# Linear attention into a routed expert layer on one core: TensorE's attention stages issued in pairs of steps, and the 1e-6 of the denominators added by ScalarE

## The chip, the core and the metric

The kernel runs on one core of a Trainium2 chip. The metric is device time in microseconds (us) of one execution; the time before the change is 609.04 us, the median of three runs (607.51 to 610.86). Five engines matter: TensorE (PE in the profile, its weight loads PEld), VectorE (DVE), ScalarE (ACT), GpSimd (POOL), and SyncE (SP), which here only issues DMAs. Each engine runs its own instructions strictly in the order in which they stand in the program; engines wait for one another through semaphores.

## The reference, cut to what matters

Inputs q, k and v are (8, 8, 576, 64): 8 batches, 8 heads, 576 rows, 64 columns. In short:

```python
def phi(x):
    proj = x @ w_phi                                  # 64 -> 128 features
    proj = proj - max(abs(proj), axis=-1)
    return concat([exp(proj), exp(-proj)])            # 256 features
q_p, k_p = phi(q), phi(k)
kv = k_p.T @ v                                        # per batch and head
z  = sum(k_p over rows)
attn = (q_p @ kv) / (q_p @ z + 1e-06)
x = attn with the heads side by side                  # (4608, 512)
do_compute = x @ w_skip > 0
expert = argmax(x @ w_gate)                           # 8 experts
out = x, and for rows with do_compute:
      x + gate * (relu(x @ w1[expert]) @ w2[expert])
```

The change lies in the attention. The expert layer follows it and is not edited.

## The kernel before, in words

**Units and items.** The work of the attention is cut into 32 units: for each of the 8 batches, two groups of four heads for k and two for q. A unit is cut into five items, numbered 0 to 4: item 0 is the last 64 rows of each head (the tail), items 1 to 4 are quarters of the other 512 rows. Two streams of 80 items, one of k and one of q, run through the same pipeline; the q stream runs 6 steps behind the k stream.

**Steps.** A loop counts steps t. In each step every stage handles the item that its lag gives. The stages are called in the order of the string `EPAZUT`, after which come the loads of v:

- T (lag 0): VectorE transposes raw rows into xT (lines 322 and 324).
- P (lag 1): TensorE multiplies xT with w_phi into ps_P (line 347). VectorE then takes the largest absolute value (354) and subtracts it (357), which gives u. ps_P has two buffers. With two full items the product is 1024 columns wide, with a tail 768.
- E (lag 3): for k, ScalarE takes the two exponentials of u (372, 373), which gives ek, and GpSimd adds parts of ek into z (380 to 386). For q, TensorE first transposes u into ps_U (393; a single buffer), and ScalarE takes the exponentials from there (399, 400).
- U (lag 4): for k, TensorE adds ek against v into ps_K (415, 422); after item 4 ScalarE copies the sum out as kvs (426). For q, TensorE multiplies the exponentials with kva into ps_O (513; the tail of odd batches at 492), and then `norm` divides: VectorE adds 1e-6 to the four denominators of a row (den, 464), takes the reciprocal (468) and multiplies twice (475, 476, tiles xm and lgm).
- Z (lag 5, item 4 of k only): TensorE sums z over the rows (433), ScalarE copies it out as zs (436).
- A (lag 6, item 4 of k only): TensorE multiplies kvs with a constant matrix that also holds the gate weights (446) and appends zs (450), in two halves; ScalarE copies each half out as kva (451, 454).

ps_O has two buffers, and the results of U, Z, the two halves of A and some small products of the router all take turns in them.

**A batch takes ten steps.** Z falls on steps that end in 4 or 9, A on those that end in 0 or 5. At a step that ends in 9 a batch of q is complete, and the router's small VectorE operations (lines 568 to 642) are queued for the steps after it.

**Who sets the order.** From step 8 to step 78 TensorE's instructions stand as the loop emits them (a manual schedule for that engine alone). The order of the other engines is set by a scheduler that plays the program through ahead of time, and the buffers of a pool are handed out by the same scheduler.

Of the kernel before, what the change touches and what calls it, by code (L numbers as in the profile page):

```python
# [12 lines left out]
AF = mybir.ActivationFunctionType  # L13
ALU = mybir.AluOpType
# [4 lines left out]
P = 128  # L19
SLOT = 256  # L20
CFG = {'late': 1, 'gp': (0, 1, 2, 4, 6, 8, 9, 11, 12, 14, 17, 19, 21), 'rows': 9.0, 'tab': (2, 4, 5, 6, 6, 7, 8, 9, 10, 11, 12, 13, 16, 20, 32), 'ql': -2, 'q1': 0, 'vtl': 3, 'at': 6, 'cp': 0, 'seq': ('E', 'E', 'E', 'C', 'C', 'SC', 'C', 'DS', 'C', 'D'), 'lag': (1, 3, 4, 5, 6), 'post': (4, 7, 7), 'man': (8, 79), 'dnow': 0, 'off': 6, 'order': 'EPAZUT', 'direct': (), 'nb': {'K': 1, 'P': 3, 'U': 2, 'O': 2}, 'na': {'K': 1, 'P': 2, 'U': 1, 'O': 2}, 'apools': (('ld', 2), ('hl', 5), ('up', 3), ('zp', 2), ('ep', 7), ('kvp', 6), ('ac', 1), ('xp', 2)), 'mpools': (('rawp', 1), ('mx', 2), ('wseta', 1), ('mo', 2), ('wsetb', 1), ('rawq', 1))}
# [3 lines left out]
def kernel(  # L25
# [12 lines left out]
    nc = tc.nc  # L38
    B, H, S, D = q.shape
    NF = w_phi.shape[1]  # L40
    E = w_gate.shape[1]
# [10 lines left out]
    NAUG = D + E + 2  # L52
    NA1 = NAUG - 1
# [80 lines left out]
    def setup_aug():  # L134
        nc.gpsimd.memset(aug, 0.0)
        for hd in range(2):
            r = slice(hd * D, (hd + 1) * D)
            c = hd * NA1
            for g in range(NP2):
                nc.gpsimd.tensor_copy(out=aug[r, g, c:c + D], in_=ident[r, hd * D:(hd + 1) * D])  # L140
            nc.gpsimd.tensor_copy(out=aug[r, :, c + D:c + NA1], in_=wgs[r])
# [114 lines left out]
    with actx:  # L256
# [17 lines left out]
        for b in range(B):  # L274
            for kind in ("k", "q"):
                for hq in range(NQ):
                    u = Unit()
# [9 lines left out]
        def st_load(u):  # L287
            src = kv_in[u.kind]
            u.raw = ld.tile([P, 2, 18, 32], F32, tag="raw", name="raw", bufs=6)
            for hd in range(2):  # L290
                for dh in range(2):
                    r = hd * 64 + dh * 32
                    nc.sync.dma_start(
                        out=u.raw[r:r + 32].rearrange("p r t c -> p (r t) c"),
                        in_=src[u.g, hd][:, :, dh * 32:dh * 32 + 32])

        def st_loadv(u):
            u.v = ld.tile([P, 4, 4 * D], F32, tag="v", name="v", bufs=3)
            u.vt = vts[u.g % 3]
            for h in range(4):  # L300
                nc.sync.dma_start(
                    out=u.v[:, h, :].rearrange("p (g c) -> p g c", c=D),
                    in_=vu[u.g, 0:4 * P, h, :].rearrange("(g p) c -> p g c", p=P))

        def st_loadvt(u):
            for pr in range(2):
                r = slice(pr * 64, pr * 64 + 64)
                nc.sync.dma_start(
                    out=u.vt[r, pr], in_=vu[u.g, 4 * P:S].rearrange("p (n r) c -> p r n c", r=2)[:, pr])
# [17 lines left out]
        def st_proj():  # L327
            todo = []
            for items, us, off in streams:
                s = now[0] - off - LP  # L330
                if 0 <= s < n:
                    todo.append(items[s])
            if not todo:
                return
            todo.sort(key=lambda x: x[1] == 0)
            p = psa.tile([P, 2, 512], F32, tag="P", name="ps_P", bufs=CFG["na"]["P"])
            nj = 0
            spans = []
            for u, i in todo:
                xT = u.hlp[0 if i == 0 else (i + 1) // 2]  # L340
                m = 1 if i == 0 else 2
                for j in range(m):
                    g = 0 if i == 0 else 2 * ((i - 1) % 2) + j
                    for hd in range(2):
                        r = slice(hd * 64, hd * 64 + 64)
                        for s in range(2):
                            nc.tensor.matmul(  # L347
                                p[s * 64:s * 64 + 64, hd, (nj + j) * NF:(nj + j + 1) * NF],
                                xT[r, g * P + s * 64:g * P + s * 64 + 64], wsrc[r], start=True, stop=True)
                spans.append((u, i, 2 * nj, 2 * (nj + m)))  # L350
                nj += m
            pv = p.rearrange("p h (j f) -> p j h f", f=NF)[:, 0:nj]
            m = small.tile([P, 8], F32, tag="m", name="m")[:, 0:2 * nj]
            nc.vector.tensor_reduce(  # L354
                out=m.rearrange("p (j h) -> p j h", h=2), in_=pv, axis=AX.X, op=ALU.max, apply_absolute_value=True)
            uu = up.tile([P, 8, NF], F32, tag="u", name="u")
            nc.vector.tensor_tensor(  # L357
                out=uu[:, 0:2 * nj, :].rearrange("p (j h) f -> p j h f", h=2), in0=pv,
                in1=m.rearrange("p (j h o) -> p j h o", h=2, o=1).broadcast_to([P, nj, 2, NF]), op=ALU.subtract)
            for u, i, a, b in spans:  # L360
                u.u[i] = uu[:, a:b, :]
# [98 lines left out]
        def norm(o, xdst, ldst, shape):  # L460

            den = small.tile([P, 4], F32, tag="den", name="den")
            rec = small.tile([P, 4], F32, tag="rec", name="rec")
            nc.vector.tensor_scalar(
                out=den.rearrange("p (t o) -> p t o", o=1), in0=o[:, :, NA1:NAUG],
                scalar1=1e-6, scalar2=None, op0=ALU.add,
            )
            nc.vector.reciprocal(out=rec, in_=den)
            rv = rec.rearrange("p (t o) -> p t o", o=1)
            a, c = shape  # L470

            def sh(x):
                return x.rearrange("p (a c) d -> p a c d", a=a)

            nc.vector.tensor_tensor(out=xdst, in0=sh(o[:, :, 0:D]), in1=sh(rv.broadcast_to([P, 4, D])), op=ALU.mult)
            nc.vector.tensor_tensor(  # L476
                out=ldst, in0=sh(o[:, :, D:NA1]), in1=sh(rv.broadcast_to([P, 4, NA1 - D])), op=ALU.mult)
# [241 lines left out]
        later = []  # L719
        now = [0]  # L720
# [5 lines left out]
        LP, LE, LU, LZ, LA = CFG["lag"]  # L726
        OFF = CFG["off"]
        streams = [(x[0], x[1], 0 if j == 0 else OFF) for j, x in enumerate(streams)]
        for dh in range(2):
            nc.scalar.dma_start(  # L730
                out=wsrc[dh * 64:dh * 64 + 64],
                in_=w_phi)
# [3 lines left out]
        def run_stage(lag, f):  # L736
            for items, us, off in streams:
                s = now[0] - off - lag
                if 0 <= s < n:
                    f(*items[s])  # L740
# [7 lines left out]
        def f_t():  # L748
            for items, us, off in streams:
                s = now[0] - off  # L750
                if s == CFG["ql"]:
                    st_load(us[0])
                if 0 <= s < n:
                    u, i = items[s]
                    st_t(u, i)
                    if i == 0 and s // 5 + 1 < len(us):
                        st_load(us[s // 5 + 1])

        man = None
        for t in range(n + OFF + LA):  # L760
            if CFG["man"] and t == CFG["man"][0]:
                man = ExitStack()
                man.enter_context(tc.manual_schedule(engines={mybir.EngineType.PE}))
            if CFG["man"] and t == CFG["man"][1]:
                man.close()
            now[0] = t
            for w, f in [x for x in later if x[0] <= t]:
                later.remove((w, f))
                f()
            for c in CFG["order"]:  # L770
                if c == "Z":
                    run_stage(LZ, st_z)
                elif c == "A":
                    run_stage(LA, st_aug)
                elif c == "U":
                    run_stage(LU, f_use)
                elif c == "E":
                    run_stage(LE, f_exp)
                elif c == "P":
                    st_proj()  # L780
                else:
                    f_t()
            run_stage(LU - 3, lambda u, i: st_loadv(u) if (i == 0 and u.kind == "k") else None)
            run_stage(CFG["vtl"], lambda u, i: st_loadvt(u) if (i == 0 and u.kind == "k") else None)
            if t == CFG["at"]:
                setup_aug()
            if t == 1:
                setup()
# [310 lines left out]
    for grp in CFG["seq"]:  # L1099
# [7 lines left out]
        for which, w, n in how:  # L1107
            for _ in range(n):
                x = slots[which]
                c = done.get((x, w), 0)  # L1110
# [6 lines left out]
    order = sorted(begin, key=begin.get)  # L1117
# [27 lines left out]
    T, ready, parted = [], [], []  # L1145
# [46 lines left out]
    with tc.manual_schedule():  # L1192
# [4 lines left out]
        for k, (w, x, c) in enumerate(steps):  # L1197
            kind, i = x
# [95 lines left out]
```

## Time and profile before

One execution was profiled. Its own time was 607.91 us, 1.1 us under the median of 609.04; its span, from the first to the last instruction, is 605.7 us, and 2.2 us lie around it.

| | |
|---|---|
| time, median of 3 runs | 609.04 us |
| time of the profiled execution | 607.91 us |
| its span | 605.7 us |
| VectorE busy | 502.6 us (83%) |
| ScalarE busy | 330.7 us (55%) |
| GpSimd busy | 375.9 us (62%) |
| attention, about | 0 to 341 us |
| steps 8 to 77, about | 25 to 301 us |

In the profile, a row of the timeline gives the start in us from the beginning of the span, the duration, the engine, the line of the kernel, the operation, the tile written and the tiles read, shapes, and how many instructions are merged in the row. A note in square brackets is idle time of that engine just before the row, and what ended it; "issue" stands for time in which the engine waited for nothing that the profile shows. For TensorE, `64*64`, `128*64`, `128*128` and `128*32` name the part of the array that a matmul uses. Matmuls overlap, so the distance between the starts of two rows says more than a duration.

### The profile page before, as it was taken

To read this page: it belongs to the slowest core of one execution; us is meant where nothing else is said; L and a number is where in the kernel's file an instruction comes from. 1 tells how busy PE (TensorE), PEld (TensorE's weight loads), DVE (VectorE), ACT (ScalarE), POOL (GpSimd) and SP (SyncE) were. 2 spreads that over 40 slices of the span, in tenths; PEclk is the share of its full clock that TensorE was granted. 3 is DMA by queue.
4 is the path that set the end of the run, shared out by engine and by line. 5 is a ranking of instruction groups with operands and counts; after the bars stand their busy time and mean duration, and the time that the engine had idled before them with its cause. 6 is when DMAs were issued, how large, how long until landed. Compare 5 with 4: busy or idle time off the path is not lost. (4 is left out here: it accounts for less than half of the span.)

```text
span 605.7 us, 18767 instructions
## 1 busy us (share of the span) xinstructions
PE 567.1 (94%) x7486; PEld 466.3 (77%) x7486; DVE 502.6 (83%) x1085; ACT 330.7 (55%) x649; POOL 375.9 (62%) x399
## 2 busy tenths in 40 slices
PE   4799999999999899998989799899999998999993
PEld 2477777777777677776766699798998987988892
DVE  5799998999999989999998749956788887867841
ACT  3366565555555565564643645344557765656720
POOL 5665585495666775847865644995576674738021
PEclk9999999999999999999999999899999999999997
DMA  9998898896677567621235297489677788868500
GB/s 159 156 164 149 182 194 179 163 211 121 149 160 155 138 135 170 158 74 46 73 120 185 69 302 277 167 278 321 201 260 240 242 288 297 269 198 261 194 19 30
DMA packets 250233, 108.33 MB, mean 179 GB/s; under 512 B 192417, under 2 KB 235553, under 8 KB 250144
## 3 DMA queue, kind: packets, MB, share of 16 engines
q1 hardware_dynamic: 245632, 97.58, 62.1%
q0 software_dynamic: 3200, 9.45, 4.3%
q8 instruction: 60, 0.98, 0.7%
q10 hardware_dynamic: 1312, 0.08, 0.1%
q14 instruction: 29, 0.24, 0.1%
HBM read 83.86 MB, written 24.02 MB: 178 GB/s over the span
## 5 line engine op out<-in xcount | busy, mean ns | idle before, releaser
L380 POOL TENSOR_TENSOR z<-ek 128x512 f32<-128x512 f32 x64 | 81.2, 1272 | 77.0 <-ACT ek L373 54.3
L200 POOL TENSOR_TENSOR w<-wraw_c,w 128x256 fp32r<-128x256 f32 x108 | 97.5, 935 | 47.5 <-ACT w L195 43.9
L195 ACT ACTIVATE w<-wraw_c 128x1024 fp32r<-128x1024 f32 x96 | 97.9, 1051 | 6.9 <-DMA wraw_c<-in_moe_w_dram 6.5
L200 DVE TENSOR_TENSOR w<-wraw_c,w 128x1024 fp32r<-128x1024 f32 x69 | 90.2, 1321 | 9.5 <-ACT w L195 7.6
L354 DVE TENSOR_REDUCE m<-ps_P 128x8 f32<-128x1024 f32 (+2 forms) x86 | 88.5, 1030 | 7.1 <-PE ps_P L347 7.1
L357 DVE TENSOR_TENSOR u<-ps_P,m 128x1024 f32<-128x1024 f32 (+2 forms) x86 | 88.8, 1032 | 2.9
L347 PE MATMUL ps_P<-wsrc,xT 64*64 64x128 f32 x2048 | 79.4, 282 | 11.4 <-DMA raw<-in_k_dram 7.2
L513 PEld LDWEIGHTS ps_O<-kva,eq 128*64 128x64 f32 x2048 | 74.0, 136 | 16.4 <-issue 5.8
L513 PE MATMUL ps_O<-kva,eq 128*64 128x74 f32 x2048 | 77.4, 228 | 3.9 <-DVE lgm L476 3.8
L347 PEld LDWEIGHTS ps_P<-wsrc,xT 64*64 64x64 f32 x2048 | 57.4, 135 | 28.1 <-issue 19.2
L399 ACT ACTIVATE eq<-ps_U 128x512 f32<-128x512 f32 x64 | 37.9, 592 | 64.8 <-PE ps_U L393 64.3
L415 PE MATMUL ps_K<-ek,v 128*64 128x256 f32 x512 | 71.2, 396 | 0.0
L879 POOL DMA_INDIRECT out_dram<-o,si x22 | 34.3, 1558 | 56.6 <-DVE si L878 50.1
L946 PE MATMUL ps_O<-w,hh 128*128 128x512 f32 x160 | 64.0, 400 | 0.0
L633 POOL TENSOR_SCALAR OP<-iota_p,rkp,wcol 128x128 bf16<-128x128 f32 x62 | 48.4, 790 | 24.0 <-DVE RKH L636 17.9
L372 ACT ACTIVATE ek<-u 128x512 f32<-128x512 f32 x64 | 40.4, 631 | 39.0 <-DVE u L357 23.0
L393 PE MATMUL ps_U<-ident,u 128*128 128x128 f32 x288 | 48.9, 287 | 2.7 <-DVE u L357 2.4
L324 DVE STREAM_TRANSPOSE xT<-raw 128x512 f32<-128x512 f32 x64 | 44.7, 702 | 6.1 <-DMA raw<-in_k_dram 3.3
L415 PEld LDWEIGHTS ps_K<-ek,v 128*64 128x64 f32 x512 | 32.0, 137 | 21.1 <-issue 10.8
L950 PE MATMUL ps_O<-w,hh 128*128 128x512 f32 x120 | 47.2, 394 | 0.1
L951 PE MATMUL ps_O<-w,hlo 128*128 128x512 f32 x120 | 47.0, 392 | 0.0
L384 POOL TENSOR_TENSOR z<-z 128x512 f32<-128x512 f32 x32 | 40.7, 1273 | 2.5
(254 smaller groups left out, 1202.0 us busy)
## 6 DMA issues: line engine op xcount, KB each, us to landing
wraw_c<-in_moe_w_dram SPq DMA_DIRECT2D x96, 512.0 KB, 5.4
raw<-in_k_dram SPq DMA_DIRECT2D x64, 144.0 KB, 3.1
raw<-in_q_dram SPq DMA_DIRECT2D x64, 144.0 KB, 4.5
v<-in_v_dram SPq DMA_DIRECT2D x64, 128.0 KB, 2.8
out_dram<-xm SPq DMA_DIRECT2D x16, 512.0 KB, 6.2
xrows<-xm SPq DMA_DIRECT2D x8, 516.0 KB, 3.8
xrows<-xm SPq DMA_DIRECT2D x8, 512.0 KB, 4.2
vt<-in_v_dram SPq DMA_DIRECT2D x32, 32.0 KB, 2.5
```

The source lines that it names most:

```text
L195: nc.scalar.activation(out=hi, in_=raw, func=AF.Copy)
L200: eng.tensor_tensor(out=lo[:, r], in0=raw[:, r], in1=hi[:, r].bitcast(F32), op=ALU.subtract)
L347: nc.tensor.matmul(p[s * 64:s * 64 + 64, hd, (nj + j) * NF:(nj + j + 1) * NF], xT[r, g * P + s * 64:g * P + s * 64 + 64], wsrc[r], start=T ...
L354: nc.vector.tensor_reduce(out=m.rearrange("p (j h) -> p j h", h=2), in_=pv, axis=AX.X, op=ALU.max, apply_absolute_value=True)
L357: nc.vector.tensor_tensor(out=uu[:, 0:2 * nj, :].rearrange("p (j h) f -> p j h f", h=2), in0=pv, in1=m.rearrange("p (j h o) -> p j h o", h ...
L380: zeng.tensor_tensor(out=z, in0=e[:, 0:2, :], in1=e[:, 2:4, :], op=ALU.add)
L393: nc.tensor.transpose(t[:, tt * P:(tt + 1) * P], uu[:, tt, :], ident)
L415: nc.tensor.matmul(o[hd * 64:hd * 64 + 64, :], u.v[:, 2 * hd + pr, g * D:(g + 1) * D], u.e[i][:, 2 * j + hd, :], start=(g == 0), stop=False,)
L513: nc.tensor.matmul(ov[s * 64:s * 64 + 64, 2 * j + hd, :], e[:, half, j, hd, s * 64:s * 64 + 64], kva[:, half, 2 * pr + hd, :], start=(half ...
L633: (nc.vector if last else nc.gpsimd).tensor_scalar(out=OP[:, t0 + t, c, :], in0=iota_p, scalar1=rkp[:, t:t + 1], scalar2=wcol[:, NT:NT + 1 ...
L946: nc.tensor.matmul(y[sub], hh[:, t], wh[:, fi, :], start=first, stop=False)
L950: nc.tensor.matmul(y[sub], hh[:, t], wl[:, fi, :], start=False, stop=False)
```

## The change

The loop still counts steps. From step 8 to step 77 it now takes two steps at once and calls their stages in the order of a list, where the number is 0 for the first step of the pair and 1 for the second (L is what a step does first, the postponed stores and router products; D the loads of v). Steps 8 and 9 are the first pair; the pairs of a batch of ten steps are called 8-9, 0-1, 2-3, 4-5 and 6-7 here, after the last digit of their steps. In `norm`, the addition of 1e-6 moves from VectorE to ScalarE.

```diff
@@ norm
-            nc.vector.tensor_scalar(
-                out=den.rearrange("p (t o) -> p t o", o=1), in0=o[:, :, NA1:NAUG],
-                scalar1=1e-6, scalar2=None, op0=ALU.add,
-            )
+            nc.scalar.activation(
+                out=den.rearrange("p (t o) -> p t o", o=1), in_=o[:, :, NA1:NAUG], func=AF.Copy, bias=1e-6)
             nc.vector.reciprocal(out=rec, in_=den)
@@ the loop over steps
+        PAIR = [('L', 0), ('T', 0), ('T', 1), ('E', 0), ('P', 0), ('P', 1), ('L', 1), ('E', 1), ('A', 0), ('Z', 0), ('Z', 1), ('U', 0), ('A', 1), ('U', 1), ('D', 0), ('D', 1)]
...
-            now[0] = t
-            for w, f in [x for x in later if x[0] <= t]:
-                later.remove((w, f))
-                f()
-            for c in CFG["order"]:
-                if c == "Z":
+            first = 8 <= t < 78 and (t - 8) % 2 == 0
+            if 8 <= t < 78 and not first:
+                continue
+            for c, dt in PAIR if first else [(c, 0) for c in "L" + CFG["order"] + "D"]:
+                now[0] = t + dt
+                if c == "L":
+                    for w, f in [x for x in later if x[0] <= now[0]]:
+                        later.remove((w, f))
+                        f()
+                elif c == "Z":
                     run_stage(LZ, st_z)
```

Below is what this makes of the order on the engines, at the places of which the prediction speaks. After the change the lines that follow `norm` have numbers lower by two (511 for 513, 490 for 492).

TensorE, steps 24 and 25 (pair 4-5), before: transposes of E (L393), products of P (L347), Z (L433), q's product of U (L513), then step 25 with E, P, the two halves of A (L446, L450) and k's product of U (L415).

```order
L393 MATMUL ps_U<-ident,u 128x128 x2
L347 MATMUL ps_P<-wsrc,xT 64x128 x16
L433 MATMUL ps_O<-z,ones_f 32x256 x4
L513 MATMUL ps_O<-kva,eq 64x74 x16
L393 MATMUL ps_U<-ident,u 128x128 x4
L347 MATMUL ps_P<-wsrc,xT 64x128 x16
L446 MATMUL ps_O<-aug,kvs 128x146 x2
L450 MATMUL ps_O<-ident,zs 128x128
L446 MATMUL ps_O<-aug,kvs 128x146 x2
L450 MATMUL ps_O<-ident,zs 128x128
L415 MATMUL ps_K<-ek,v 64x256 x4
```

The same two steps on TensorE after:

```order
L393 MATMUL ps_U<-ident,u 128x128 x2
L347 MATMUL ps_P<-wsrc,xT 64x128 x32
L393 MATMUL ps_U<-ident,u 128x128 x4
L433 MATMUL ps_O<-z,ones_f 32x256 x4
L511 MATMUL ps_O<-kva,eq 64x74 x16
L446 MATMUL ps_O<-aug,kvs 128x146 x2
L450 MATMUL ps_O<-ident,zs 128x128
L446 MATMUL ps_O<-aug,kvs 128x146 x2
L450 MATMUL ps_O<-ident,zs 128x128
L415 MATMUL ps_K<-ek,v 64x256 x4
```

The products of both steps stand side by side, and nothing but q's product of U is left between Z and A; before, E and P of the next step stood there.

VectorE, steps 24 and 25, before (the numbers tell buffers apart; ps_P_2188 is the product of step 24, ps_P_2256 that of step 25):

```order
L354 TENSOR_REDUCE m_2205<-ps_P_2188 128x8
L324 STREAM_TRANSPOSE xT_2518<-raw_1935 128x512
L357 TENSOR_TENSOR u_2207<-ps_P_2188,m_2205 128x1024
L464 TENSOR_SCALAR den_2233<-ps_O_2216 128x4
L468 RECIPROCAL rec_2234<-den_2233 128x4
L475 TENSOR_TENSOR xm_1995<-ps_O_2216,rec_2234 128x4x64
L476 TENSOR_TENSOR lgm_1997<-ps_O_2216,rec_2234 128x2x18
L324 STREAM_TRANSPOSE xT_2606<-raw_2008 128x512
L354 TENSOR_REDUCE m_2273<-ps_P_2256 128x8
L357 TENSOR_TENSOR u_2275<-ps_P_2256,m_2273 128x1024
```

VectorE, the same steps after (ps_P_2197 is the product of step 24, ps_P_2218 that of step 25):

```order
L354 TENSOR_REDUCE m_2214<-ps_P_2197 128x8
L324 STREAM_TRANSPOSE xT_2455<-raw_1881 128x512
L324 STREAM_TRANSPOSE xT_2457<-raw_1890 128x512
L357 TENSOR_TENSOR u_2216<-ps_P_2197,m_2214 128x1024
L354 TENSOR_REDUCE m_2235<-ps_P_2218 128x8
L357 TENSOR_TENSOR u_2237<-ps_P_2218,m_2235 128x1024
L466 RECIPROCAL rec_2279<-den_2278 128x4
L473 TENSOR_TENSOR xm_2004<-ps_O_2261,rec_2279 128x4x64
L474 TENSOR_TENSOR lgm_2006<-ps_O_2261,rec_2279 128x2x18
```

Two transposes stand between the reduction and the subtraction of the first product, and den is gone from this engine.

ScalarE, steps 24 and 25, before (zs is Z's copy, eq and ek are exponentials, kva the copies of A's halves; u_2207 comes from the product of step 24):

```order
L436 ACTIVATE zs_2214<-ps_O_2209 128x256
L399 ACTIVATE eq_2253<-ps_U_2248 128x512
L400 ACTIVATE eq_2253<-ps_U_2248 128x512
L372 ACTIVATE ek_2321<-u_2207 128x4x128
L373 ACTIVATE ek_2321<-u_2207 128x4x128
L451 ACTIVATE kva_2277<-ps_O_2278 128x4x73
L454 ACTIVATE kva_2277<-ps_O_2278 128x4
L451 ACTIVATE kva_2277<-ps_O_2284 128x4x73
L454 ACTIVATE kva_2277<-ps_O_2284 128x4
```

ScalarE, the same steps after (u_2216 comes from the product of step 24):

```order
L399 ACTIVATE eq_2251<-ps_U_2246 128x512
L400 ACTIVATE eq_2251<-ps_U_2246 128x512
L436 ACTIVATE zs_2259<-ps_O_2254 128x256
L372 ACTIVATE ek_2332<-u_2216 128x4x128
L373 ACTIVATE ek_2332<-u_2216 128x4x128
L464 ACTIVATE den_2278<-ps_O_2261 128x4
L451 ACTIVATE kva_2284<-ps_O_2285 128x4x73
L454 ACTIVATE kva_2284<-ps_O_2285 128x4
L451 ACTIVATE kva_2284<-ps_O_2291 128x4x73
L454 ACTIVATE kva_2284<-ps_O_2291 128x4
```

The new den stands between ek and the copies of A. The second half of A (ps_O_2291) now takes the buffer that the first half (ps_O_2285) leaves, and waits for ScalarE's copy of the first; before, it took the buffer of q's product of U and waited for VectorE's line 476.

ScalarE, steps 40 and 41 (pair 0-1), before (u_2552 comes from the product of step 39):

```order
L372 ACTIVATE ek_2696<-u_2552 128x4x128
L373 ACTIVATE ek_2696<-u_2552 128x4x128
L451 ACTIVATE kva_2644<-ps_O_2645 128x4x73
L454 ACTIVATE kva_2644<-ps_O_2645 128x4
L451 ACTIVATE kva_2644<-ps_O_2651 128x4x73
L454 ACTIVATE kva_2644<-ps_O_2651 128x4
L573 ACTIVATE ex_2587<-d_2586 128x32
```

ScalarE, the same steps after (u_2658 comes from the product of step 40 itself):

```order
L571 ACTIVATE ex_2587<-d_2586 128x32
L399 ACTIVATE eq_2688<-ps_U_2683 128x512
L400 ACTIVATE eq_2688<-ps_U_2683 128x512
L451 ACTIVATE kva_2691<-ps_O_2692 128x4x73
L454 ACTIVATE kva_2691<-ps_O_2692 128x4
L372 ACTIVATE ek_2776<-u_2658 128x4x128
L373 ACTIVATE ek_2776<-u_2658 128x4x128
L451 ACTIVATE kva_2691<-ps_O_2698 128x4x73
L454 ACTIVATE kva_2691<-ps_O_2698 128x4
```

The copy of A's second half now stands behind exponentials of the pair's own first product. The first matmuls that need this copy are those of line 490 where the step has a tail of q, else those of line 511 in the second step.

More of the change, by code (lines that the diff above doesn't have):

```diff
@@ L780 @@
                     st_proj()
+                elif c == "D":
+                    run_stage(LU - 3, lambda u, i: st_loadv(u) if (i == 0 and u.kind == "k") else None)
+                    run_stage(CFG["vtl"], lambda u, i: st_loadvt(u) if (i == 0 and u.kind == "k") else None)
                 else:
                     f_t()
-            run_stage(LU - 3, lambda u, i: st_loadv(u) if (i == 0 and u.kind == "k") else None)
-            run_stage(CFG["vtl"], lambda u, i: st_loadvt(u) if (i == 0 and u.kind == "k") else None)
             if t == CFG["at"]:
```

## The prediction

> **What bounds the kernel now.** I read the page's busy shares first, then the windows view of ten steps in the middle of the attention, then TensorE's timeline there, the grouped waits on TensorE, and last the timelines of VectorE and ScalarE.
>
> The page's line of busy times, and the windows row of ten steps; its columns are the window, its length, and the busy time (with the count) of TensorE, its weight loads, VectorE, ScalarE and GpSimd, then clock, DMA share and GB/s:
>
> ```profile
> PE 567.1 (94%) x7486; PEld 466.3 (77%) x7486; DVE 502.6 (83%) x1085; ACT 330.7 (55%) x649; POOL 375.9 (62%) x399
> 220.00:260.00 40.00, 40.00 (x783) 31.38 (x775) 37.74 (x95) 23.50 (x56) 26.50 (x24) 1.00 0.62 139
> ```
>
> TensorE has no idle time in this window. VectorE, at 37.74 of 40, is nearly as full, ScalarE is not. So in the attention a TensorE instruction saved is time saved, until VectorE or a wait takes over. Transposes that open ten steps, from the timeline:
>
> ```profile
> 251.03 0.63 PE L393 MATMUL ps_U<-ident,u 128*128 128x128 f32 x4
> 291.13 0.64 PE L393 MATMUL ps_U<-ident,u 128*128 128x128 f32 x4
> ```
>
> Ten steps take 40.10 us here. Batches alternate: those whose q tail runs in line 492 have it in pairs 0-1 and 4-5 (Y below), the others (X) have no such line there, and a larger block of router work. This is an X. The grouped waits (sum, count, mean, in us) show what stops TensorE:
>
> ```profile
> PE ps_O L513 <- DVE lgm L476: 3.8, 3, 1.3
> PE ps_O L609 <- DVE lgm L476: 2.2, 3, 0.7
> ```
>
> Three of each: one pair of stalls in each X, none in Y.
>
> **Part 1: fewer changes between parts of the array.** A stretch of the weight loads, from A in pair 0-1 to the products of pair 2-3, with the notes of idle time before them:
>
> ```profile
> 187.26 0.55 PEld L446 LDWEIGHTS ps_O<-aug,kvs 128*128 128x128 f32 x4 [0.17 <-issue]
> ...
> 192.30 1.26 PEld L513 LDWEIGHTS ps_O<-kva,eq 128*64 128x64 f32 x32
> 193.64 0.42 PEld L393 LDWEIGHTS ps_U<-ident,u 128*128 128x128 f32 x4
> 194.22 0.43 PEld L347 LDWEIGHTS ps_P<-wsrc,xT 64*64 64x64 f32 x16 [0.17 <-issue]
> 194.61 0.26 PEld L347 LDWEIGHTS ps_P<-wsrc,xTt 64*64 64x64 f32 x8
> 195.04 0.63 PEld L415 LDWEIGHTS ps_K<-ek,v 128*64 128x64 f32 x8 [0.17 <-issue]
> ```
>
> Entering and leaving `64*64` costs .17 each, and so does entering A. From `128*64` to `128*128` it is 193.64 − (192.30 + 1.26) = .08. Two steps before, each E, P, U: 2 × .08 + 4 × .17 = .84. The pair E, P, P, E, U, U: .08 + 3 × .17 = .59. Saved .25. Where A stands in the pair, one change more or less goes with it: .42 in pair 0-1 (A follows E directly), .17 in pair 4-5. Over five pairs the mean is (3 × .25 + .42 + .17)/5 = .27. There are 35 pairs: −9.4 us, all on the path, since TensorE is never idle there.
>
> The Trainium skill, page "TensorEngine Tiling (Array Packing)", section "Key Properties", says that a change of tiling mode drains TensorE. The rows at .17 agree, the one at .08 agrees only in half. If each change cost a whole gap, two would go per pair: 2 × .17 × 35 = 11.9, and the sum below would be 2.5 lower.
>
> **Part 2: X's stalls go.** TensorE's rows of the two stalls:
>
> ```profile
> 277.81 0.19 PE L609 MATMUL ps_O<-Stot,ones_b 128*128 128x40 bf16 x1 [0.73 <-DVE lgm L476]
> 285.38 1.25 PE L513 MATMUL ps_O<-kva,eq 128*64 128x74 f32 x32 [1.27 <-DVE lgm L476]
> ```
>
> Both wait for a ps_O buffer that VectorE's norm holds. In pairs the two products of U follow each other and the next use of ps_O comes after a new E, P, P, E, so 3 × (.73 + 1.27) = 6.0 goes; I leave .4 per X for the router's products, which now meet VectorE's small operations at another place. −4.8, bounds −6.0 and −3.
>
> **Part 3: a new wait in every pair 4-5 (place 1).** TensorE's timeline has the durations (start, duration):
>
> ```profile
> 262.42 0.44 PE L393 MATMUL ps_U<-ident,u 128*128 128x128 f32 x2
> 262.79 1.10 PE L347 MATMUL ps_P<-wsrc,xT 64*64 64x128 f32 x32
> 263.82 0.64 PE L433 MATMUL ps_O<-z,ones_f 128*32 128x256 f32 x8
> 264.39 1.25 PE L513 MATMUL ps_O<-kva,eq 128*64 128x74 f32 x32
> 265.57 0.66 PE L393 MATMUL ps_U<-ident,u 128*128 128x128 f32 x4
> 266.16 1.10 PE L347 MATMUL ps_P<-wsrc,xT 64*64 64x128 f32 x32
> 267.19 0.77 PE L446 MATMUL ps_O<-aug,kvs 128*128 128x146 f32 x4
> 267.79 0.27 PE L450 MATMUL ps_O<-ident,zs 128*128 128x128 f32 x1
> 267.90 0.73 PE L446 MATMUL ps_O<-aug,kvs 128*128 128x146 f32 x4
> ```
>
> By distances between starts, and without its entry gap for a second product, TensorE arrives at the second half of A after E .37, P 1.03 and .86, E .47, Z .55, U 1.18, first half .72: 5.2 us into the pair. That half needs the buffer of the first, thus ScalarE's copies of it, which stand behind the exponentials of the pair's own first product and behind den. VectorE and ScalarE rows for that chain:
>
> ```profile
> 285.15 1.22 DVE L354 TENSOR_REDUCE m<-ps_P 128x8 f32<-128x1024 f32 x1
> 286.28 0.70 DVE L324 STREAM_TRANSPOSE xT<-raw 128x512 f32<-128x512 f32 x1
> 286.90 1.19 DVE L357 TENSOR_TENSOR u<-ps_P,m 128x1024 f32<-128x1024 f32 x1
> 288.01 0.14 DVE L464 TENSOR_SCALAR den<-ps_O 128x4 f32<-128x4 f32 x1
> 288.19 0.18 DVE L468 RECIPROCAL rec<-den 128x4 f32<-128x4 f32 x1
> 288.40 0.42 DVE L475 TENSOR_TENSOR xm<-ps_O,rec 128x256 f32<-128x256 f32 x1
> 288.74 0.18 DVE L476 TENSOR_TENSOR lgm<-ps_O,rec 128x36 f32<-128x36 f32 x1
> 288.84 0.70 DVE L324 STREAM_TRANSPOSE xT<-raw 128x512 f32<-128x512 f32 x1
> ```
>
> ```profile
> 267.29 0.63 ACT L372 ACTIVATE ek<-u 128x512 f32<-128x512 f32 x1
> 267.81 0.63 ACT L373 ACTIVATE ek<-u 128x512 f32<-128x512 f32 x1
> 268.33 0.41 ACT L451 ACTIVATE kva<-ps_O 128x292 f32<-128x292 f32 x1
> 268.63 0.19 ACT L454 ACTIVATE kva<-ps_O 128x4 f32<-128x4 f32 x1
> 268.78 0.41 ACT L451 ACTIVATE kva<-ps_O 128x292 f32<-128x292 f32 x1
> ```
>
> The first product is done at .37 + 1.10 = 1.47. Then reduction 1.13, two transposes 1.24 (they now stand between), subtraction 1.11, exponentials 1.04, den .16, copy .45, and three handoffs at an estimated .1 (the stall's row at 285.38 starts .16 after lgm's end at 285.22): 1.47 + 5.13 + .3 = 6.9. The wait is 6.9 − 5.2 = 1.7, if VectorE is on time. It can be late: with den gone it has 37.7 − 1.4 = 36.3 us of work in ten steps, TensorE 40.0 − 2.7 = 37.3 (2.7 are five pairs at .27, and the X stalls go besides), so a lateness is hardly made up; I allow up to one reduction, 1.1. Floor 1.4 (no handoff), bounds 1.4 to 2.8. I take 1.9, near the floor, because each wait gives VectorE time. Seven pairs: +13.3, bounds 9.8 and 19.6.
>
> **Part 4: a new wait in pair 0-1 (place 2).** The copy of A's second half stands on ScalarE behind ek of the pair's first product (both exponentials in Y, one in X, by the order). Counted from the end of the first product of pair 8-9, TensorE needs that copy after: product .86, E .37, Z .57, U 1.35 + 1.13 + 1.13 (with k's tail in line 422), E .59, the products 1.03 + .65, E .5, both halves of A 1.35, U of k .92: 10.5, for line 492 in Y. In X the first user is line 513 of the second step, 1.35 later: 11.8. VectorE from the same point: two reductions and subtractions 4.6, transposes 2 × .62, two norms without den 1.3 (.65 each), the router's reduction and two small operations .93, reduction 1.13, two small ones .3, transpose .62, subtraction 1.11: 11.2. The router's part is from this row and from the reciprocal's:
>
> ```profile
> 268.29 0.63 DVE L568 TENSOR_REDUCE L<-lgm 128x36 f32<-128x288 f32 x1
> ```
>
> Then exponentials 1.04 (X .52) and a copy .45: 12.8 in Y, 12.3 in X, so waits of 2.3 and .5. With VectorE on time (the product of pair 0-1 itself at 7.2, then 1.13 + .3 + .62 + 1.11 + 1.04 + .45 = 4.65) it would be 1.3 and 0; from the other side, one late reduction more, 3.4 and 1.6. Three of each, the first pair 0-1 has no router work and no q: 3 × 2.3 + 3 × .5 = +8.4, bounds 3.9 and 15.
>
> **Part 5: den.** Its group before, and the nearest row for it on ScalarE (sum, mean ns):
>
> ```profile
> L464 DVE TENSOR_SCALAR den<-ps_O 128x4 f32<-128x4 f32 x72 | 11.0, 153 | 3.1 <-PE ps_O L492 1.4 <-PE ps_O L513 1.1
> L454 ACT ACTIVATE kva<-ps_O 128x4 f32<-128x4 f32 x32 | 5.7, 179 | 0.0
> ```
>
> VectorE loses 72 × .18 (start to start) = 13 us of work; that is in the 36.3 and 11.2 above and is not counted again. ScalarE gains 72 × .16 to .18, about 1.3 us in ten steps, with 16 idle: hidden, except in place 1. The reciprocal now waits for another engine: +.2 to .3 where VectorE had nothing else to do, which VectorE's queue covers. GpSimd (26.5 of 40) and the loads of v, now at the pair's end, are not late by their rows: 0.
>
> **Sum** against the profiled 607.91: −9.4 − 4.8 + 13.3 + 8.4 = +7.5, or 615.4. That execution lies 1.1 under the median of 609.04, so on the median's scale 616.5.
>
> **Rivals.**
>
> *Faster: TensorE's waits feed VectorE.* VectorE loses 13 us, and waits let it run ahead. If it is on time everywhere and handoffs overlap, place 1 is 1.4 × 7 = 9.8, place 2 vanishes because ScalarE's copy comes before line 492 wants it, and the gaps go at a whole .17: −11.9 − 4.8 + 9.8 = −6.9, or 602. For it: the 16 idle us of ScalarE, and that TensorE has no reserve it could lose. Against it: place 1's chain starts at the pair's own product, so its 1.4 doesn't depend on VectorE's lead. It decides by whether the subtraction of the first product ends before TensorE reaches A's second half.
>
> *No change.* VectorE on time at the small gaps: −9.4 − 4.8 + 11.9 (1.7 × 7) + 3.9 = +1.6, or 610.6; with X's stalls wholly gone, 609.4. For it: these are the floors of the two chains.
>
> *Slower still: den queued behind exponentials.* In pair 2-3 and others ScalarE has ek of the next product ahead of den, and ek waits for VectorE's subtraction. If that makes each norm late by .4 (half a pair of exponentials, rows at 267.29) in 35 pairs, 14 us more: 630. Against it: VectorE's subtraction stands ahead of the reciprocal too.
>
> That the change doesn't do what it says is excluded by the order, which shows the pairs and den on ScalarE.
>
> **How the numbers follow.** Forecast case, both places waiting, 612 (both at the floors of the no-change case and a little over) to 624 (place 1 at 2.8 in all pairs, which gives 622.8, and place 2 a little over its value): .47, value 616.5. Slower still: .11. No change: .18. Faster: .24. A difference under about 0.5%, 3.0 us, can't be told from none in this kernel, so faster .24, same .18, slower .58. The range 600 to 628 leaves out about .1 of the faster case's lower part (whole gaps and place 1 under its floor) and .08 above.
>
> **What would show it.** In the profile after: weight loads of line 347 with two .17 gaps per pair and not four (part 1); no waits of L609 and L511 on lgm (part 2); on TensorE L446 or L450 in pair 4-5 waiting 1.4 to 2.8 for kva, L454, seven times (part 3); L490 in Y waiting 1.3 to 3.4 for kva in pair 0-1, L511 in X at most 1.6 (part 4); VectorE's busy time 11 lower and ScalarE's about 12 higher (part 5); ten steps of X about 40.0, of Y about 41 to 43. If place 1 waits less than 1 us, the chain was drawn wrong and the sum turns to the faster side; if the reciprocal (L466) waits for den in most pairs, the slower rival holds.

## The result, and the profile after

The changed kernel takes 637.52 us (median of 4 runs, 636.85 to 641.12), the kernel before 608.27 us beside it (607.24 to 610.86). The ratio is 1.0486, with a 95% interval of 1.0433 to 1.0539: 29 us slower. The forecast was 616.5 us in a range of 600 to 628. The profiled span went from 605.7 to 635.0 us, 29.3 more.

The page of after, busy times and TensorE's granted clock in 40 slices:

```profile
PE 571.1 (90%) x7486; PEld 476.1 (75%) x7486; DVE 493.5 (78%) x1013; ACT 339.7 (53%) x721; POOL 373.5 (59%) x399
PEclk9799998999899989899999969999999999999998
```

The same row of clocks before:

```profile
PEclk9999999999999999999999999899999999999997
```

VectorE lost 9.1 us of work, ScalarE gained 9.0, TensorE's instructions are the same in number, and each engine's share of the span is smaller: what grew is waiting. And where the attention had a full clock throughout, six slices up to its end now show less. The grouped waits of after (sum, count, longest):

```profile
PE ps_O L446 <- ACT kva L454: 12.0, 7, 2.2
PE ps_O L490 <- ACT kva L454: 10.0, 6, 2.6
PE ps_O L511 <- ACT kva L454: 5.7, 3, 1.9
PE ps_O L511 <- DVE lgm L474: 5.8, 2, 5.3
```

The first row is place 1, seven times; the second and third are place 2, in Y (two waits, .76 and 2.59, 3.35 together, three times) and in X (1.90, three times). The fourth has the .46 that follows the pairs and one wait of 5.35 at the end of the attention, which no step of the prediction names. X's six stalls of before are gone. Ten steps, from the transposes that open pair 6-7:

```profile
101.14 0.63 PE L393 MATMUL ps_U<-ident,u 128*128 128x128 f32 x4
141.58 0.63 PE L393 MATMUL ps_U<-ident,u 128*128 128x128 f32 x4
187.19 0.64 PE L393 MATMUL ps_U<-ident,u 128*128 128x128 f32 x4
```

The X batch takes 40.44 us here (40.10 before), the Y batch 45.61 (39.83 before). This X comes out as the terms say: its waits of 1.90 and 1.75, less the two stalls (2.0 together) and five gaps of .24, leave +.45, and +.34 is measured. Y has 4.9 us of waits and grew by 5.8, although gaps were saved. The next X, whose wait at place 1 is 2.21 with a stretch at half clock behind it, takes 42.93 (its successor opens at 230.12).

### The profile page after: what moved, and what is told of

Its sections match the earlier page's. It is cut to its first block, busy times and chain, and to the rows that moved or that the text cites. A ratio compares the mean times of both kernels' runs of the same rounds, so it can differ in the third digit from the quotient of the medians.

```text
span 635.0 us, 18812 instructions
## 1 busy us (share of the span) xinstructions
PE 571.1 (90%) x7486; PEld 476.1 (75%) x7486; DVE 493.5 (78%) x1013; ACT 339.7 (53%) x721; POOL 373.5 (59%) x399
## 5 line engine op out<-in xcount | busy, mean ns | idle before, releaser
L200 POOL TENSOR_TENSOR w<-wraw_c,w 128x256 fp32r<-128x256 f32 x108 | 99.0, 948 | 53.0 <-ACT w L195 52.9
L200 DVE TENSOR_TENSOR w<-wraw_c,w 128x1024 fp32r<-128x1024 f32 x69 | 91.8, 1345 | 13.5 <-ACT w L195 13.1
L511 PEld LDWEIGHTS ps_O<-kva,eq 128*64 128x64 f32 x2048 | 76.9, 139 | 24.4 <-issue 6.2
L511 PE MATMUL ps_O<-kva,eq 128*64 128x74 f32 x2048 | 80.6, 231 | 12.8 <-DVE lgm L474 5.8
L347 PE MATMUL ps_P<-wsrc,xT 64*64 64x128 f32 x2048 | 75.7, 284 | 12.8 <-DVE xT L324 6.8
L347 PEld LDWEIGHTS ps_P<-wsrc,xT 64*64 64x64 f32 x2048 | 60.0, 138 | 24.1 <-issue 16.0
L415 PE MATMUL ps_K<-ek,v 128*64 128x256 f32 x512 | 74.3, 411 | 0.0
L883 POOL DMA_INDIRECT out_dram<-o,si x22 | 31.1, 1415 | 58.2 <-DVE si L882 51.7
L415 PEld LDWEIGHTS ps_K<-ek,v 128*64 128x64 f32 x512 | 35.5, 144 | 20.2 <-issue 10.0
L393 PE MATMUL ps_U<-ident,u 128*128 128x128 f32 x288 | 49.7, 291 | 0.0
```

The source lines that it names most:

```text
L200: eng.tensor_tensor(out=lo[:, r], in0=raw[:, r], in1=hi[:, r].bitcast(F32), op=ALU.subtract)
L347: nc.tensor.matmul(p[s * 64:s * 64 + 64, hd, (nj + j) * NF:(nj + j + 1) * NF], xT[r, g * P + s * 64:g * P + s * 64 + 64], wsrc[r], start=T ...
L393: nc.tensor.transpose(t[:, tt * P:(tt + 1) * P], uu[:, tt, :], ident)
L415: nc.tensor.matmul(o[hd * 64:hd * 64 + 64, :], u.v[:, 2 * hd + pr, g * D:(g + 1) * D], u.e[i][:, 2 * j + hd, :], start=(g == 0), stop=False,)
L511: nc.tensor.matmul(ov[s * 64:s * 64 + 64, 2 * j + hd, :], e[:, half, j, hd, s * 64:s * 64 + 64], kva[:, half, 2 * pr + hd, :], start=(half ...
```

## The experiments

Each kernel was compared with the kernel before on the same chip; ratios are with their 95% intervals. The theory after the result: the waits at places 1 and 2, spells at half clock behind them (a spell is a stretch in which TensorE's granted clock is half), and den behind other work on ScalarE at the end. The rivals were that den on ScalarE is the cause all through (A), that VectorE was the bound and lacks something (B), that den is free (C), and that a wait taken away only moves to the next place (D).

### The two parts apart

Pairs with den on VectorE, which takes the lines of `norm` back:

```diff
-            nc.scalar.activation(
-                out=den.rearrange("p (t o) -> p t o", o=1), in_=o[:, :, NA1:NAUG], func=AF.Copy, bias=1e-6)
+            nc.vector.tensor_scalar(
+                out=den.rearrange("p (t o) -> p t o", o=1), in0=o[:, :, NA1:NAUG],
+                scalar1=1e-6, scalar2=None, op0=ALU.add,
+            )
```

> Pairs as in the change, den back on VectorE. Theory (waits of the pairs plus half-clock spells behind them): the waits at places 1 and 2 stay at 1.6 to 1.8 and, by batch, 3.3 and 1.9 us, and only the 5.35 us before the last line-511 matmuls goes: about 631 us. Rival A (den queued on ScalarE makes the copies and norms late): most of the 29 us goes, 612 or under. Rival B (VectorE was the bound and den's 13 us are missing again): 645 or over.

Measured: 632.91 us, ratio 1.0417 (1.037 to 1.0464). Its grouped waits:

```profile
PE ps_O L446 <- ACT kva L454: 10.4, 7, 1.9
PE ps_O L492 <- ACT kva L454: 10.0, 6, 2.6
PE ps_O L513 <- ACT kva L454: 5.7, 3, 1.9
```

Place 2 waits as with the whole change, place 1 a little less (10.4 against 12.0). The pairs alone make 24.4 of the 29 us; rivals A and B fall for the pairs.

The other half, the single steps of before with only `norm` changed as in the diff of the change:

> Steps one by one as before, den alone on ScalarE. Theory: the attention to step 77 takes the same within 3 us (the six stalls on lgm change by some tenths), and den stands behind four weight conversions of 3.9 us on ScalarE at the end of the attention: +5 to +7, about 615 us. Rival A: 625 or over. Rival C (den is free, since ScalarE has room): 608 us, within 3 us.

Measured: 629.11 us, ratio 1.0324 (1.0283 to 1.0365). That is far over the theory's 615 and in rival A's range: with single steps den on ScalarE costs 20.6 us, and the two halves don't add up to the whole (45.0 against 29.3). The place is the step of Z. ScalarE, VectorE and TensorE of this kernel there:

```profile
300.19 0.63 ACT L372 ACTIVATE ek<-u 128x512 f32<-128x512 f32 x1 [2.67 <-DVE u L357]
300.73 0.61 ACT L373 ACTIVATE ek<-u 128x512 f32<-128x512 f32 x1
301.25 0.15 ACT L464 ACTIVATE den<-ps_O 128x4 f32<-128x4 f32 x1
301.43 0.18 DVE L466 RECIPROCAL rec<-den 128x4 f32<-128x4 f32 x1 [1.33 <-ACT den L464]
302.39 1.43 PE L511 MATMUL ps_O<-kva,eq 128*64 128x74 f32 x32 [2.52 <-DVE lgm L474]
```

Den takes .15 us, but stands behind two exponentials, before which ScalarE waited 2.67 for VectorE's subtraction. VectorE, done with that subtraction, then waits 1.33 for ScalarE, and TensorE waits 2.52 for the buffer that the norm holds (1.27 before, in X; in Y, where there was none, 2.03). The other steps of Z have seven new waits of .56 on Z's copy. This is the prediction's rival of den behind exponentials, in the kernel that has no pairs.

Den on ScalarE only up to step 77, first with the pairs, then with single steps; the edit is the same in both:

```diff
+            if now[0] < 78:
+                nc.scalar.activation(
+                    out=den.rearrange("p (t o) -> p t o", o=1), in_=o[:, :, NA1:NAUG], func=AF.Copy, bias=1e-6)
+            else:
+                nc.vector.tensor_scalar(
+                    out=den.rearrange("p (t o) -> p t o", o=1), in0=o[:, :, NA1:NAUG],
+                    scalar1=1e-6, scalar2=None, op0=ALU.add,
+                )
```

> The changed kernel, but from step 78 on VectorE adds the 1e-6 again. Theory: only the wait of 5.35 us before the last line-511 matmuls goes: 631 to 632 us. Rival: the experts' first weights set the start of the next part and the time stays at 637 us.

Measured: 632.66 us, ratio 1.0399 (1.0358 to 1.0441); 4.9 us of the change's time lie in den at the end. From there to den wholly on VectorE (632.91) there is no difference clear of the noise: up to step 77 den costs no time that shows in the pairs. The rows of the changed kernel show why the end is not:

```profile
363.71 3.89 ACT L195 ACTIVATE w<-wraw_c 128x1024 fp32r<-128x1024 f32 x4
367.50 0.23 ACT L464 ACTIVATE den<-ps_O 128x4 f32<-128x4 f32 x2
367.63 1.75 DVE L200 TENSOR_TENSOR w<-wraw_c,w 128x1024 fp32r<-128x1024 f32 x1 [4.48 <-ACT w L195]
369.31 0.23 DVE L466 RECIPROCAL rec<-den 128x4 f32<-128x4 f32 x2
370.25 2.24 PE L511 MATMUL ps_O<-kva,eq 128*64 128x74 f32 x32 [5.35 <-DVE lgm L474]
```

And the same place before:

```profile
338.51 3.90 ACT L195 ACTIVATE w<-wraw_c 128x1024 fp32r<-128x1024 f32 x4
338.67 0.16 DVE L464 TENSOR_SCALAR den<-ps_O 128x4 f32<-128x4 f32 x1 [0.70 <-PE ps_O L513]
```

Before, VectorE made den while ScalarE converted the experts' weights for 3.9 us. Now den stands behind that conversion, and the reciprocal behind a part of the conversion on VectorE as well.

> Single steps, den on ScalarE up to step 77 and on VectorE after it. Theory: of den's price with single steps, 4.9 us lie at the end (den behind the weight conversions), the rest at the steps of Z, where den stands behind exponentials that wait for VectorE, and in half-clock spells behind these waits: about 624 us. Rival: the end is worth most of it, 612 us or under.

Measured: 622.17 us, ratio 1.0236 (1.0203 to 1.027), so the end is not worth most of it: of den's 20.6 us with single steps about 7 lie at the end, and 13.7 before it.

### The pairs with A as single steps

One pair or both are left out by their digit:

```diff
-            first = 8 <= t < 78 and (t - 8) % 2 == 0
-            if 8 <= t < 78 and not first:
+            paired = 8 <= t < 78 and t % 10 not in (0, 1)
+            first = paired and t % 2 == 0
+            if paired and not first:
                 continue
```

With (0, 1), pair 0-1 is two single steps:

> The changed kernel with the pair 0-1 issued as two single steps again. Theory: the waits of place 2 go (3 x 3.35 + 3 x 1.90 = 15.8 us) and three half-clock spells behind them (about 1.8 us each, 5.4), 7 x 0.35 us of gaps comes back: about 619 us, and no spell at half clock is left in pairs 0-1. Rival D (a wait only moves: TensorE then stalls as long at the next place, since VectorE is the bound): 632 us or over. Without the clock's share it would be 624 us.

Measured: 639.94 us, ratio 1.0501 (1.0458 to 1.0543). Nothing is gained, as rival D had it, and its grouped waits say where the gain went:

```profile
PE ps_O L446 <- ACT kva L454: 15.0, 7, 2.2
PE ps_P L347 <- DVE u L357: 8.8, 8, 1.8
PE ps_O L511 <- DVE rm L625: 3.8, 6, 0.9
PE ps_O L490 <- ACT kva L454: 2.5, 3, 0.8
```

Of place 2's 15.8 us 2.5 are left, but place 1 waits 3.0 longer, the products wait for u 2.8 longer (8.8 against 6.0), and line 511 waits for the router's rm 3.3 longer (.54 in the changed kernel). The gaps of seven pairs (2.5) and 1.2 of waits on eq come to that: 12.8 of 13.3. And there are six spells at half clock as with the change, now behind place 1. So a place has no price of its own here. The rows fit a VectorE that used the wait to catch up; no run shows that apart.

With (4, 5) in the same line, pair 4-5 is two single steps:

> The changed kernel with the pair 4-5 issued as two single steps. Simple theory (each place has its price): the 12.0 us of place 1 and the half-clock spells behind it go, 7 x 0.15 us of gaps comes back: about 624 us. Rival D, which the same cut at pair 0-1 favoured (the wait moves to the next place): 634 to 640 us, with new waits of line 511 on lgm or rm.

Measured: 628.87 us, ratio 1.0315 (1.0279 to 1.035), 8.7 us better than the change. The time lies between the simple sum (624) and rival D (634 or more). By the rows the simple sum is nearer: the waits of place 1 are gone and place 2 stays as it was, while line 511 waits once, near the end, 3.5 for the router's cs on VectorE (.73 with the change), with a spell behind it; and two of the three spells behind place 2 in Y last twice as long as with the change.

With (0, 1, 4, 5), and den on VectorE:

> Den on VectorE, pairs only at 6-7, 8-9 and 2-3; the pairs with A stand as single steps. Theory (the copies of A behind the pair's own exponentials are what costs): no wait on kva over 1 us, gaps save 7 x 0.67 = 4.7 us, the six stalls on lgm may stay: 604 to 608 us. Rival D (pairs make VectorE late wherever they stand): waits on u, rm or lgm in the single steps behind them, 613 us or over.

Measured: 609.91 us, ratio 1.0015 (1.0004 to 1.0027), between the theory's 608 and rival D's 613. Against 632.91 for all five pairs with den on VectorE, the two pairs with A cost 23.0 us together, more than either by itself gave back. Between them stand the smaller waits of rival D (.93 and .35 in each X, .83 in each Y); they replace the 2.0 in X. Line 513 waits 3.4 for the router's cs once, at the pairs' end.

The pair turned round, with den on VectorE:

```diff
+        PAIR = [('L', 0), ('T', 0), ('T', 1), ('A', 0), ('Z', 0), ('U', 0), ('E', 0), ('P', 0), ('P', 1), ('L', 1), ('Z', 1), ('E', 1), ('A', 1), ('U', 1), ('D', 0), ('D', 1)]
```

> Den on VectorE; the pair is turned: A, Z, U of the first step, then E, P, P, Z, E, A, U, with as many changes between parts of the array as in the change. In pair 0-1 both copies of A stand ahead of the pair's exponentials. Theory: place 2 goes wholly, place 1 at least halves, the gaps' 7.7 us stay saved: 602 to 610 us. Rival D: VectorE is late at another place instead, 615 us or over.

Measured: 632.2 us, ratio 1.0372 (1.0351 to 1.0392). The waits on kva fell to 7.2 us in all, but 20.9 us of waits on zs, Z's copy on ScalarE, came instead. Rival D again.

### The half clock

The third Y batch of the changed kernel, in windows of 4 us (busy times as in the prediction, the third number from the end is the granted clock):

```profile
246.00:250.00 4.00, 3.54 (x50) 2.59 (x42) 3.96 (x8) 2.58 (x7) 2.19 (x2) 1.00 0.91 146
250.00:254.00 4.00, 1.11 (x25) 0.96 (x27) 4.00 (x10) 1.76 (x6) 0.98 (x1) 1.00 1.16 247
254.00:258.00 4.00, 4.00 (x52) 3.96 (x50) 1.25 (x5) 0.79 (x3) 2.83 (x3) 0.57 0.70 199
```

TensorE is busy for 1.11 of 4 us because of place 2's waits, and then runs without a pause at a clock of .57 on average. To tell whether the wait brings the spell, the wait was filled with useless matmuls, behind the second half of A in steps 20, 40 and 60; they write columns that nobody reads:

```diff
                 nc.tensor.transpose(a[:, 4 * NA1:4 * NA1 + P], u.zs[:, f], ident)
+                if half == 1 and now[0] in (20, 40, 60):
+                    for x in range(20):
+                        nc.tensor.matmul(a[:, 420:512], ident, u.kvs[:, 0, 0:92], start=True, stop=True)
```

> The changed kernel with 20 useless matmuls on TensorE behind the second half of A in pairs 0-1 of the three Y batches, 1.8 us of work each time, less than the wait that follows. Clock theory (a spell at half clock follows a stretch with too much waiting): the wait of 2.59 us shrinks by that much, the three spells at half clock behind it vanish, and the time falls by 3 x 1.5 to 1.8 to about 632.5 us although TensorE does more. Rival (the clock falls for another reason): the three spells stay and the time is 637.5 us or more.

Measured: 640.24 us, ratio 1.0519 (1.0501 to 1.0536). The three spells vanished, but 20 of these matmuls take 4.6 us and not 1.8, and hold up the copy of A by 1.8, so the time tells nothing. With `range(9)` in the same line:

> As the filled kernel before it, with 9 useless matmuls in place of 20: each took 0.23 us there, not the 0.09 reckoned with, and 4.6 us of them held up the copy of A. Nine take 2.1 us and end before ScalarE reaches that copy. Clock theory: the copy of A comes at the same time as in the changed kernel, the waits of 0.76 and 2.59 us shrink to under 1.5 together, the three spells at half clock in pairs 0-1 of Y are gone, and ten Y steps take 1.5 to 1.8 us less, 4.5 to 5.4 in all: about 632.5 us if no new spell comes elsewhere. Rival: the spells stay, 637.5 us.

Measured: 633.24 us, ratio 1.0428 (1.0391 to 1.0465): 4.3 us less than the change, with more work on TensorE. The two intervals overlap a little, so the rows have to decide. The second Y batch in the changed kernel, from the end of place 2's wait to the next pair:

```profile
164.69 1.11 PE L490 MATMUL ps_O<-kva,eqt 128*64 128x74 f32 x25 [2.59 <-ACT kva L454]
...
165.72 1.91 PE L415 MATMUL ps_K<-ek,v 128*64 128x256 f32 x7
...
169.73 0.66 PE L393 MATMUL ps_U<-ident,u 128*128 128x128 f32 x4
```

And filled with nine (line 493 is line 490 there):

```profile
163.38 1.05 PE L493 MATMUL ps_O<-kva,eqt 128*64 128x74 f32 x25 [1.59 <-ACT kva L457]
...
164.33 1.03 PE L415 MATMUL ps_K<-ek,v 128*64 128x256 f32 x7
...
166.75 0.66 PE L393 MATMUL ps_U<-ident,u 128*128 128x128 f32 x4
```

The same instructions take 5.04 us there and 3.37 here: a spell costs 1.67. In the first and third Y batch the spell is gone as well, and the wait ends no earlier than in the changed kernel. Outside these three places both kernels have four spells up to step 77, though not all at the same places. So the wait left unfilled brings these three spells.

### A version that is faster than both

The pairs without A, and only where neither the start nor the end of the attention is in them, den on VectorE. First the three pairs 6-7, 8-9 and 2-3:

```diff
+            paired = 16 <= t < 76 and t % 10 not in (0, 1, 4, 5)
+            first = paired and t % 2 == 0
+            if paired and not first:
                 continue
```

> Pairs 6-7, 8-9 and 2-3 only, den on VectorE, and only from step 16 to step 75, so that the start and the end of the attention are as before. From the run with these pairs to step 77: 79.0 us for twenty steps against 79.9, over sixty steps 2.8 us less: 605.5 to 607 us, faster than before. Rival: the first pair's half-clock spell and the late router products only move: 608 to 611 us.

Measured: 606.9 us against 608.46, ratio 0.9976 (0.9961 to 0.9991), as the theory had it.

Then, with (0, 1, 2, 3, 4, 5) in that line, pairs 6-7 and 8-9 only:

> The same with the pairs 6-7 and 8-9 only, from step 16 to step 75. Saved gaps: 6 x (0.32 + 0.10) = 2.5 us. If the waits on u and on kva in the single steps behind the pairs come from pair 2-3, they go, and it is as fast as with three pairs or faster, 604 to 607 us; if they come from pair 8-9 (the copy of A in step 0 stands behind its exponentials), they stay and the time is 607 to 610 us.

Measured: 606.44 us, ratio 0.9963 (0.9946 to 0.998). The time is in the first case's range, but the copy of A in the single step 0 comes .84 too late in Y here too, so that wait is from pair 8-9, as the second case had it; the one of .93 in X came from pair 2-3. By the intervals both versions are a little faster than before, by .1% to .54%, which is about or under the half per cent that the prediction calls no difference; the two can't be told apart. The second one's waits:

```profile
PE ps_O L492 <- ACT kva L454: 2.5, 3, 0.8
PE ps_O L513 <- DVE lgm L476: 1.7, 3, 0.6
...
149.94 1.48 PE L492 MATMUL ps_O<-kva,eqt 128*64 128x74 f32 x32 [0.84 <-ACT kva L454]
...
229.10 1.48 PE L492 MATMUL ps_O<-kva,eqt 128*64 128x74 f32 x32 [0.84 <-ACT kva L454]
```

Twenty steps take 79.16 us, against 79.93 (40.10 and 39.83) before.

## Why the prediction was wrong

The sign and both places were right; the size was off by 22 us on the scale of the spans (+7.5 against +29.3), and the time lies above the range and beyond the rival that was to be slower still. Three steps failed: waits were priced without the half clock behind them (no term, about 10.5 us), place 2 was sized too small (8.4, measured 15.8), and den was taken as hidden (0, measured 4.9 at the end).

- **Gaps (−9.4).** Held. Free of waits and spells, pair 6-7 takes 6.98 us after against 7.30, pair 8-9 7.14 against 7.24, pair 0-1 in X 7.65 against 8.00, pair 2-3 in Y 7.35 against 7.66, and pair 4-5 .05 less in Y and .23 in X. The mean is .24 and the sum −8.5. The Trainium skill's rule of a drain at each change ("TensorEngine Tiling (Array Packing)", "Key Properties") would have given 11.9 by whole gaps; the measured sum doesn't bear that out.
- **X's stalls (−4.8).** Held: −6.0, with one .54 for the router in the place of the three .4.
- **Place 1 (+13.3).** Held: seven waits of 1.56 to 2.21, 12.0 in all, within the bounds of 9.8 to 19.6.
- **Place 2 (+8.4, bounds 3.9 to 15).** The mechanism held, the term was mis-sized: 15.8. The part of the term that failed is "the router's reduction and two small operations .93", which leaves .15 for each of the two. X in the changed kernel, with the VectorE operation that subtracts the router's maximum (line 570), GpSimd, and what follows on ScalarE and VectorE (rows between these are left out):

```profile
204.27 1.26 POOL L380 TENSOR_TENSOR z<-ek 128x512 f32<-128x512 f32 x1 [0.39 <-PE ps_U L393]
204.30 1.29 DVE L570 TENSOR_TENSOR d<-L,mx 128x40 f32<-128x40 f32 x1
205.62 0.24 ACT L571 ACTIVATE ex<-d 128x40 f32<-128x40 f32 x1 [1.43 <-DVE d L570]
206.72 0.41 ACT L451 ACTIVATE kva<-ps_O 128x292 f32<-128x292 f32 x1
207.48 1.18 DVE L357 TENSOR_TENSOR u<-ps_P,m 128x1024 f32<-128x1024 f32 x1
208.75 0.63 ACT L372 ACTIVATE ek<-u 128x512 f32<-128x512 f32 x1 [1.55 <-DVE km L577]
209.29 0.40 ACT L451 ACTIVATE kva<-ps_O 128x292 f32<-128x292 f32 x1
```

  A tiny operation, 40 elements in each row, takes 1.29 us instead of .15. The subtraction of the product ends at 208.66; counted from the end of pair 8-9's first product (195.9) that is 12.8 and not 11.2, in Y as in X, and line 570 is 1.1 of the 1.6; the rest was not traced. In Y, as here in X, the operation also holds ScalarE up before ex (1.43 in the row), which puts the copy of A's first half late too: the .76 that the prediction didn't have.
- **Den (0).** "Hidden, except in place 1" failed: 4.9 us at the end, where the row it should have been checked against, four conversions on ScalarE of 3.9 us together, stands in the trace of before. The prediction looked at ScalarE's idle share in ten steps and not at its queue after step 78. The rival that priced den behind exponentials gave it 14 us in the pairs; with the pairs no time shows for it up to step 77, with single steps 13.7.
- **Half clock (no term).** The prediction added waits as if each cost only itself. To step 77 the profile of after has seven spells at half clock, the first of them, at the start, twice as long as the others; that of before has none. What the other terms leave, 29.3 − (−8.5 − 5.4 + 12.0 + 15.8 + 4.9) = 10.5 us, is about seven times the 1.67 measured (11.7). The filled waits show this for the three in Y; for the other four it is only worked out.

What a wait must be like to bring a spell is only partly settled: in the changed kernel place 1's wait of 2.21, the one of 1.76 and one of the three of 1.56 have a spell behind them, X's of 1.90 at place 2 have none, but one of the same 1.90 has in the kernel filled with nine. It matters how a wait falls against a fixed grid of time, as the last section shows. Nor was it tried to take GpSimd's addition away from beside line 570 in the paired kernel.

## What to carry to other kernels

When steps of one engine are gathered, follow each result through the in-order queues of the others: what the first half of the pair produces now stands ahead of what its second half needs, and the gather costs more in that chain than it saves in switches. Price a small operation by what stands ahead of it on its new engine at every place where it occurs, the last ones too, and not by the engine's idle share. And price a wait of TensorE in a stretch that runs at full clock with the half-clock spell that may follow it, 1.67 us here for 3.35 of waiting.

## What the runs showed of the hardware

TensorE's clock fell to half for about 3.4 us behind waits of 1.6 to 3.4 us in otherwise full work. The clock records of all fourteen kernels show more than the windows of 4 us above: within a run, every change of the clock lies a multiple of 3.413 us from every other, and a spell inside the kernel fills one stretch of this grid, or two or three in a row. Between 30 and 330 us, each of the 28 stretches at full clock in which TensorE was busy for less than .43 of the time has a spell behind it, and none with .55 or more has; in between both occur. So a wait counts by how it falls on the grid. In the changed kernel the 2.21 at place 1 lies in one stretch, which leaves TensorE busy for 1.21 of 3.41 us, and a spell follows; the 1.75 falls across two, of which the emptier is busy for 2.16, and none follows. The 1.90 in X leaves 1.51 both where a spell follows and where none does, so this busy time is not the whole measure.

The Trainium skill, page "TensorE: Matmul & The Clock Gate", section "Part 1: The HAM clock gate", describes a clock gate that passes half of the pulses after an idle window of about 3.4 us. The half clock and the length of the spells agree; the waits here were shorter than such a window, and TensorE worked 1.11 of the 4 us before a spell.

A VectorE operation with two inputs lasted until the GpSimd operation that was running when it started had ended. The group of line 570 after (sum, mean ns):

```profile
L570 DVE TENSOR_TENSOR d<-L,mx 128x32 f32<-128x32 f32 (+1 forms) x8 | 7.8, 969 | 0.2
```

and of the same operation before:

```profile
L572 DVE TENSOR_TENSOR d<-L,mx 128x32 f32<-128x32 f32 (+1 forms) x8 | 1.5, 191 | 0.0
```

In the quoted X, line 570 ends at 205.59 and GpSimd's addition, started .03 earlier, at 205.53. With another start the end follows the addition all the same: in the kernel with the pairs alone the operation starts .34 to .36 us after the addition and takes .96 to .97, in the turned pair .70 to .73 after it and takes .59 to .62, and each time it ends .04 to .06 behind it. Up to step 77 of the single steps, with den on VectorE or on ScalarE, no addition runs beside it, and it takes .18 to .19. The Trainium skill, page "SBUF — State Buffer", section "SBUF: two separate sides", says that VectorE with two SBUF inputs and GpSimd take a shared pair of ports for a whole instruction, and that the other one waits. The rows agree; that the order of the change brought the two together is seen in the trace, and no run kept the pairs and took the addition away.
